# First Mlp products, its input and its first weights around the end of a planned attention stage

## The chip, the cores and the metric

The kernel runs on one core of a Trainium2 chip. The metric is the device time of one execution in microseconds (us). A core has a matrix engine (TensorE, here PE, with its weight loads shown apart as PEld), three elementwise engines (VectorE is DVE, ScalarE is ACT, GpSimd is POOL), SyncE (SP), which issues most transfers, and 16 DMA engines that carry them. Each engine runs its own instructions in order and waits for others by semaphores.

## The reference, cut to what matters

```python
q, k, v: (4, 8, 768, 48);  beta: (4, 8, 768)              # fp32
k_n = k / (norm(k) + 1e-6)
for t in range(768):                                       # delta rule, per batch and head
    y[t]  = q[t] @ state
    state = state + beta[t] * outer(k_n[t], v[t] - k_n[t] @ state)
x = y as (3072 tokens, 384)
h = x @ w_in                       # Mlp 1, 384 -> 2048
P = a0 + a1*h + a2*h^2 + a3*h^3
Q = 1 + |b0|*|h| + |b1|*h^2
x = (P / (Q + 1e-6)) @ w_out       # 2048 -> 384
h = x @ w_in2                      # Mlp 2
out = (h * tanh(log1p(exp(h)))) @ w_out2
```

## The kernel before

**Attention** goes through the 768 positions in 12 units of 64 tokens. A unit needs the inverse of a triangular 64x64 matrix per batch and head, which is reduced to 32x32 blocks; one inversion serves a pair of units, and is named here by its odd unit (1, 3, 5, 7, 9, 11). `inverse` makes it: a transposition on DVE (L534), a multiplication by rows (L538), thirty steps of one product (L552) and one addition (L558), a multiplication by columns (L580), and a second transposition on DVE (L586). `ON_DVE = (1, 9)` puts the multiplications and steps of two inversions on DVE, the other four on POOL. `prepare` loads a unit, normalises k (L449), transposes (L383), makes the Gram matrices (L398, L419) and masks them (L407, L429); L466 sets the inversion's input. `step(u)` is the recurrence itself, on the critical chain: products on PE (L690, L707, L728, L736, L751), copies out of PSUM on ACT (L714, L719, L744, L760), the rest on DVE (L698). The last products of a unit (L751) are copied (L760) and stored to `x1` by ACT's queue (L806).

**Weights.** Each Mlp has 16 blocks of 128 hidden features. An fp32 weight is split into a high and a low part for three fp32r products. A block has two sides (`w_in`, `w_out`), and each side is fetched raw (L841), then goes through `mag` on ACT (L852), `size`, `sign`, `low` on DVE (L856, L861, L867), `out` on ACT (L874) and `rest`, a subtraction on POOL (L879). A converted block is stored to DRAM (L908) and fetched again in the Mlp (L911); blocks 0 and 1 of Mlp 1 (`FQ = 2`) stay in SBUF. All 16 blocks of Mlp 1 are converted within attention.

**The plan.** Attention, the conversion, and the Mlp's first input are given to `Plan` as operations with an engine, a cost, what they read and what they write. `Plan.order` is a list scheduler: whenever an engine is free it takes the ready operation with the longest tail. `Plan.best` repeats it 2500 times with random additions to the tail of each kind of operation and keeps the best. The order found is the order of the instructions on every engine. Where the plan has a gap on PE, products of zeros are put in (L1239).

**The Mlps** run over 96 units each: 6 groups of 512 tokens (4 batches x 128 positions) by 16 blocks. `up` is nine matmuls into a PSUM bank `h` (L999); the rational function goes over ACT (L1061, L1068, L1070, L1081, L1083, L1010), DVE (L1088 to L1106) and POOL (L1064, L1074, L1014); `down` is nine matmuls four units later (L1025). The order within a unit is a written list. Group 0's input is fetched from `x1` and split into high (ACT, L979) and low (POOL, L983) parts at the end of the plan. Before the loop five blocks (`LOOK = 5`) are fetched. The conversion of eight blocks of Mlp 2 (`DIRECT = 8`) runs in Mlp 1's units by `Conv.pull`, one pull being one operation on DVE with what belongs to it on ACT, POOL and SP; its first three raw loads (`conv.start`) are issued at unit 3.

Of the kernel before, what the change touches and what calls it, by code (L numbers as in the profile page):

```python
# [9 lines left out]
F32 = mybir.dt.float32  # L10
# [12 lines left out]
HB = 16  # L23
# [3 lines left out]
DIRECT = 8  # L27
LOAD = 2700
# [17 lines left out]
CONV_START, CONV_RATE = 6, 4  # L46
# [22 lines left out]
class Plan:  # L69
# [31 lines left out]
    def order(self, bias=None):  # L101

        n = len(self.ops)
        tail, then, left = [0] * n, [[] for _ in range(n)], [0] * n
        for i in range(n - 1, -1, -1):
            engine, ns, fn, need, more, early = self.ops[i]
            tail[i] += ns + more
            left[i] = len(need)
            for j in need:
                then[j].append(i)  # L110
                tail[j] = max(tail[j], tail[i] + self.HOP)
        tail = [t - self.ops[i][5] + (bias or {}).get(self.kinds[i], 0) for i, t in enumerate(tail)]
        ready = {}
        for i in range(n):
            if not left[i]:
                ready.setdefault(self.ops[i][0], []).append((0, i))
        free, at, done = {}, [0] * n, []
        while any(ready.values()):
            best = None
            for engine, queue in ready.items():  # L120
                if queue:
                    t = max(free.get(engine, 0), min(r for r, _ in queue))
                    if best is None or t < best[0]:
                        best = (t, engine)
            t, engine = best
            queue = ready[engine]
            pick = max((x for x in queue if x[0] <= t), key=lambda x: (tail[x[1]], -x[1]))
            queue.remove(pick)
            i = pick[1]
            end = t + self.ops[i][1]  # L130
            free[engine] = end
            done.append((t, end, i))
            for j in then[i]:
                left[j] -= 1
                at[j] = max(at[j], end + self.ops[i][4] + (0 if self.ops[j][0] == engine else self.HOP))
                if not left[j]:
                    ready.setdefault(self.ops[j][0], []).append((at[j], j))
        return done

    TRIALS = 2500  # L140

    def best(self):

        def end(order):
            return max(e for _, e, _ in order)
        self.kinds = [(op[0], names[0].strip("0123456789") if names else "") for op, names in zip(self.ops, self.names)]
        kinds, rng = sorted(set(self.kinds)), random.Random(0)
        bias, order = {}, self.order()
        for _ in range(self.TRIALS):
            trial = dict(bias)  # L150
            for k in rng.sample(kinds, rng.choice((1, 2, 4))):
                trial[k] = trial.get(k, 0) + rng.gauss(0, rng.choice((1000, 5000, 20000)))
            other = self.order(trial)
            if end(other) <= end(order):
                bias, order = trial, other
        return order
# [19 lines left out]
class Attention:  # L176
# [4 lines left out]
    def __init__(self, ctx, tc, q, k, v, beta, x1, spare, spare_x):  # L181
# [17 lines left out]
        self.whole, = ring("whole", 1, [128, 2 * C])  # L199
        part, = ring("part", 1, [128, 3])  # L200
        self.top, self.bot, self.low = (part[:, i:i + 1] for i in range(3))
        self.kn = ring("kn", self.NKN, [128, M, DP])
        self.lz, self.vz = self.kn[6:]
# [9 lines left out]
        self.tmp = [flat[:, 2 * M * HC + 256 * i:2 * M * HC + 256 * i + 256] for i in range(2)]  # L213
# [1150 lines left out]
```

## Time and profile before

| | us |
|---|---|
| median of 3 runs (1089.65 to 1092.43) | 1092.06 |
| the profiled execution | 1098.82 |
| its span (first to last instruction) | 1097.1 |
| attention, to the end of its last product | 300.06 |
| first Mlp unit after which PE is without a gap | from 318.30 |

Times inside the execution count from the start of the span; 1.7 us lie outside it. In the profile's rows an instruction has its start, its duration, its engine and line, what it writes and reads, and in brackets how long the engine had been idle and what ended that.

### The profile page before, as it was taken

The numbers are of one execution on the slowest core, as the hardware profiler recorded it, in microseconds if no ns is written. First come the engines' busy times: TensorE is split into PE (matmuls) and PEld (weight loads), VectorE is DVE, ScalarE is ACT, GpSimd is POOL, SyncE is SP. The second block draws the span as 40 slices with busy tenths as digits, with TensorE's granted clock in tenths as the row PEclk, the third lists the DMA queues.
The fourth block names the chain that finished last, engine by engine and source line by source line (L and its number), as shares of the span: only waits on it lengthen the run. The fifth ranks groups of instructions, "written<-read, shape, count | busy, mean of one in ns | idle before, by whom it ended". The sixth has DMA issues, their size and how long they took to land.

```text
span 1097.1 us, 24930 instructions
## 1 busy us (share of the span) xinstructions
PE 1049.6 (96%) x10228; PEld 895.5 (82%) x10228; DVE 686.7 (63%) x1154; ACT 605.0 (55%) x1081; POOL 553.0 (50%) x640
## 2 busy tenths in 40 slices
PE   7988889988889999999999999999999999999998
PEld 6988878877768888888888888888888888888897
DVE  6886658785369999999999999882222222222211
ACT  4534645324478888989889898643232322323222
POOL 4388998186268888787888888763000000000000
PEclk9998989889899999999999999999999999999999
DMA  8727875057691121211203046340101102011010
GB/s 127 139 63 182 223 201 138 10 152 218 220 362 70 39 78 43 84 47 73 87 15 104 13 144 245 101 145 1 28 30 15 43 2 57 1 22 36 10 20 29
DMA packets 152947, 99.25 MB, mean 90 GB/s; under 512 B 114048, under 2 KB 136192, under 8 KB 152832
## 3 DMA queue, kind: packets, MB, share of 16 engines
q1 hardware_dynamic: 150976, 96.77, 31.1%
q8 instruction: 80, 1.31, 0.5%
q10 hardware_dynamic: 1600, 0.79, 0.2%
q0 software_dynamic: 256, 0.10, 0.1%
q14 instruction: 35, 0.29, 0.1%
HBM read 66.16 MB, written 31.46 MB: 89 GB/s over the span
## 4 chain that ended last, share of the span: by engine, by line
PE 83%; DVE 7%; issue 3%; POOL 3%; ACT 1%; SPq 1%; DMA 1%; DVEq 0%; POOLq 0%; ACTq 0%
PE h L999 35%; PE o L1025 33%; PE o L1039 3%; PE c_ps L707 3%; PE y_ps L751 3%; DVE xraw L552 2%; PE c_ps L728 1%; PE c_ps L690 1%; PE t_ps L383 1%; SPq L252 1%; PE s_all L736 1%; DVE s_all L558 1%; POOL x L558 1%; PE t_ps L398 1%; DVE x L558 1%
## 5 line engine op out<-in xcount | busy, mean ns | idle before, releaser
L999 PE MATMUL h<-x,w 128*128 128x512 f32 x1728 | 426.4, 391 | 4.1 <-DVE s L1090 1.9
L1025 PE MATMUL o<-gh,w 128*128 128x512 f32 x1584 | 387.6, 389 | 0.0
L999 PEld LDWEIGHTS h<-x,w 128*128 128x128 f32 x1728 | 325.0, 188 | 73.8 <-DVE s L1090 3.0
L1025 PEld LDWEIGHTS o<-gh,w 128*128 128x128 f32 x1584 | 297.3, 188 | 61.7
L1121 ACT ACTIVATE gh<-h 128x512 fp32r<-128x512 f32 x96 | 57.5, 599 | 263.1 <-PE h L999 263.1
L1014 DVE TENSOR_TENSOR gh<-g,gh 128x512 fp32r<-128x512 f32 x80 | 55.0, 687 | 232.4 <-ACT g L1126 232.4
L1014 POOL TENSOR_TENSOR gh<-g,gh 128x512 fp32r<-128x512 f32 x112 | 145.4, 1299 | 67.4 <-ACT gh L1010 45.7
L1074 POOL TENSOR_TENSOR q<-q,r 128x512 f32<-128x512 f32 x96 | 131.8, 1373 | 29.9 <-ACT r L1068 25.1
L1088 DVE TENSOR_TENSOR s<-s,h 128x512 f32<-128x512 f32 x96 | 65.3, 681 | 27.7 <-ACT s L1070 17.0
L1070 ACT ACTIVATE s<-h,ab 128x512 f32<-128x512 f32 x96 | 74.0, 771 | 5.1 <-PE h L999 5.1
L1061 ACT ACTIVATE q<-h 128x512 f32<-128x512 f32 x96 | 57.5, 599 | 35.0 <-PE h L999 34.8
L1090 DVE SCALAR_TENSOR_TENSOR s<-s,ab,h 128x512 f32<-128x512 f32 x96 | 71.8, 748 | 3.4
L1101 DVE SCALAR_TENSOR_TENSOR r<-s,ab,r 128x512 f32<-128x512 f32 x96 | 71.8, 748 | 0.0
L1106 DVE SCALAR_TENSOR_TENSOR g<-q,r 128x512 f32<-128x512 f32 x96 | 66.0, 687 | 3.3
L1081 ACT ACTIVATE r<-q,cst 128x512 f32<-128x512 f32 x96 | 66.1, 688 | 1.7 <-POOL q L1074 1.7
L558 POOL TENSOR_TENSOR x<-x,xraw 128x30 f32<-128x30 f32 (+14 forms) x120 | 62.2, 518 | 9.4
L1097 DVE SCALAR_TENSOR_TENSOR q<-q,r 128x512 f32<-128x512 f32 x96 | 65.3, 680 | 0.9 <-ACT r L1083 0.6
L879 POOL TENSOR_TENSOR w<-wm,w 128x384 fp32r<-128x384 f32 x48 | 49.6, 1037 | 32.0 <-ACT w L874 23.7
L552 POOL TENSOR_TENSOR xraw<-x 128x30 f32<-128x30 f32 (+14 forms) x120 | 60.2, 502 | 7.3
L1010 ACT CAST gh<-g 128x512 fp32r<-128x512 f32 x96 | 59.1, 616 | 0.5 <-DVE g L1106 0.5
L1083 ACT ACTIVATE r<-r 128x512 f32<-128x512 f32 x96 | 55.9, 582 | 3.1
L1126 ACT ACTIVATE g<-h 128x512 f32<-128x512 f32 x96 | 57.0, 594 | 0.0
(139 smaller groups left out, 1283.5 us busy)
## 6 DMA issues: line engine op xcount, KB each, us to landing
w<-w SPq DMA_DIRECT2D x36, 768.0 KB, 6.9
w<-in_moe_w_in_dram SPq DMA_DIRECT2D x32, 384.0 KB, 3.7
w<-in_moe_w_out_dram SPq DMA_DIRECT2D x32, 384.0 KB, 3.6
xraw<-x SPq DMA_DIRECT2D x36, 256.0 KB, 4.1
w<-wt SPq DMA_DIRECT2D x8, 768.0 KB, 3.5
kn<-in_k_dram SPq DMA_DIRECT2D x48, 96.0 KB, 3.8
qn<-in_q_dram SPq DMA_DIRECT2D x48, 96.0 KB, 4.2
v<-in_v_dram SPq DMA_DIRECT2D x48, 96.0 KB, 3.4
```

The costliest lines, as they stand in the source:

```text
L552: eng.tensor_tensor(out=tv, in0=ls[:, j, j + 1:HC].unsqueeze(1).to_broadcast([128, j, n]), in1=xs[:, 0:j, j:j + 1].to_broadcast([128, j, n ...
L558: eng.tensor_tensor(out=xs[:, 0:j, j + 1:HC], in0=xs[:, 0:j, j + 1:HC], in1=tv, op=ALU.add)
L999: self.nc.tensor.matmul(out=self.st[i]["h"], lhsT=self.w.t[f][:, a, 0, k], rhs=self.x[g][:, b, k], start=(n == 0), stop=(n == 8),)
L1014: (nc.gpsimd if engine == "P" else nc.vector).tensor_tensor(out=s["gh"][:, 1], in0=s["g"], in1=s["gh"][:, 0].bitcast(F32), op=ALU.subtract)
L1025: self.nc.tensor.matmul(out=self.acc[g][d], lhsT=self.w.t[f][:, a, 1, d], rhs=self.st[i]["gh"][:, b], start=(first and n == 0), stop=(last ...
L1070: nc.scalar.activation(out=s["s"], in_=s["h"], func=ACTF.Identity, scale=k["a3"], bias=k["a2"])
L1074: nc.gpsimd.tensor_tensor(out=s["q"], in0=s["q"], in1=s["r"], op=ALU.mult)
L1081: nc.scalar.activation(out=s["r"], in_=s["q"], func=ACTF.Ln, bias=k["c"])
L1088: nc.vector.tensor_tensor(out=s["s"], in0=s["s"], in1=s["h"], op=ALU.mult)
L1090: nc.vector.scalar_tensor_tensor(out=s["s"], in0=s["s"], scalar=k["a1"], in1=s["h"], op0=ALU.add, op1=ALU.mult)
L1101: nc.vector.scalar_tensor_tensor(out=s["r"], in0=s["s"], scalar=k["a0"], in1=s["r"], op0=ALU.add, op1=ALU.mult)
L1106: nc.vector.scalar_tensor_tensor(out=s["g"], in0=s["q"], scalar=2.0, in1=s["r"], op0=ALU.subtract, op1=ALU.mult, reverse0=True)
```

## The change

1. `Plan.best` is gone. `Plan.order` runs once, with a written table `BIAS` that is added to the tails: an entry for a kind of operation on an engine, and further ones for the same kind in one twelfth of the program.
2. The two PSUM banks of attention's `t_ps` are now the Mlp's two `h` banks, and `up` of units 0 and 1 (18 matmuls) is part of the plan, six operations of three matmuls.
3. Group 0's input no longer shares SBUF with the state copies `U`, but with the inversions' work tiles (`xs`, `tmp`), so `x_hi` and `x_lo` may run ahead of attention's end.
4. `DEFER = 2`: blocks 14 and 15 of Mlp 1 are neither converted nor stored in attention. `Conv` converts them in the Mlp's units 0 to 10 (12 pulls) straight into the tiles that the products read; its first raw loads are issued right behind the five fetches. Mlp 2's conversion starts at unit 11.
5. A way of inverting by 16x16 blocks that nothing used (`SPLIT = ()`) is removed, with its set-up: two large memsets on DVE and copies and selections of masks on POOL.

```diff
-CONV_START, CONV_RATE = 6, 4
+CONV_START, CONV_RATE = 11, 4
+BIAS = {
+    "ACT:S": -174504, "ACT:S:2": -124989, "ACT:S:3": 62305, "ACT:S:4": 130858, "ACT:S:5": 21268, "ACT:S:6": 144220,
...
+        rank = [
+            t - op[5] + BIAS.get(kind, 0) + BIAS.get(f"{kind}:{i * 12 // n}", 0)
+            for i, (t, op, kind) in enumerate(zip(tail, ops, kinds))
+        ]
...
-        for t, end, i in self.best():
+        for t, end, i in self.order():
...
-        for t in (self.vz, self.lz, *self.su):
+        for t in self.su:
             nc.vector.memset(t, 0.0)
...
+    ps.add(ctx.enter_context(tc.tile_pool(name="ps1", bufs=1, space=PSUM)), h=2)
...
-    conv = Conv([w2.convert(f, side) for f in range(NF) for side in range(2)])
+    conv = Conv(
+        [w1.convert(f, side) for f in range(NF - DEFER, NF) for side in range(2)]
+        + [w2.convert(f, side) for f in range(NF) for side in range(2)]
+    )
...
-        w1.plan(plan, [*range(FQ, NF), *range(FQ)])
+        w1.plan(plan, [*range(FQ, NF - DEFER), *range(FQ)])
...
-            plan.add("ACT", 620, lambda n=n: m1.x_hi(0, n), ["xr"], [f"x{n}", "xs0", "xs1", "U0", "U1"], early=late)
+            plan.add("ACT", 620, lambda n=n: m1.x_hi(0, n), ["xr"], [f"x{n}", "xs0", "xs1", "tmp0", "tmp1"], early=late)
             plan.add("POOL", 1300, lambda n=n: m1.x_lo(0, n), (), [f"x{n}"], early=late)
+        for n in range(2):
+            fns = m1.up(n, 0, n)
+            for j in range(0, 9, 3):
+                plan.add("PE", 690, lambda fns=fns[j:j + 3]: run(fns), [f"x{k}" for k in range(3)] + [f"w{n}"], [f"t{n}"], early=late)
...
-        fetch_w = {n: (w1.fetch_split, FQ + LOOK + n) for n in range(NF - FQ - LOOK)}
+        fetch_w = {n: (w1.fetch_split, FQ + LOOK + n) for n in range(NF - DEFER - FQ - LOOK)}
...
         for f in range(LOOK):
             w1.fetch_split(FQ + f)
+        w1.word = None
+        conv.start()
...
-        ups, downs = {}, {}
+        ups, downs = {0: [], 1: []}, {}
...
-            if i == CONV_START - 3:
-                conv.start()
...
+                elif op == "c" and i < CONV_START:
+                    conv.pull(6 * DEFER * (i + 1) // CONV_START - conv.n)
```

The lines move: `mag` is L773 after the change, `rest` L800, the raw fetch L762, the block fetch L832, `up` L920, the Mlp's `s`, `q`, `r` L991, L982, L989, its Ln and Exp L1002, L1004, the inversion's rows, steps and columns L542, L551 and L557, L561, `kn` L467, attention's y products and uu products L672 and L628.

**ACT at the start of the Mlp.** In ACT's order before, the copy and stores of the last attention output (not shown) are followed by the elementwise work of units 0, 1 and 2 (`s`, `q`, `r` from the bank `h`):

```order
L1070 ACTIVATE s<-h,ab 128x512 [waits PE_49]
L1061 ACTIVATE q<-h 128x512
L1068 ACTIVATE r<-q,ab 128x512 [waits Activation_49]
L1070 ACTIVATE s<-h,ab 128x512 [waits PE_49]
L1061 ACTIVATE q<-h 128x512
L1081 ACTIVATE r<-q,cst 128x512 [waits Pool_49]
L1083 ACTIVATE r<-r 128x512 [waits Activation_49]
```

Now, from the copy of the last attention output and its two stores on (`yst`, `x_5_65`):

```order
L681 COPY yst_159<-y_ps_164 128x8x64 [waits PE_49]
L727 DMA x_5_65<-yst_159 48x8x128 [waits Activation_49]
L727 DMA x_5_65<-yst_159 48x8x128
L991 ACTIVATE s<-h,ab 128x512
L982 ACTIVATE q<-h 128x512
L989 ACTIVATE r<-q,ab 128x512 [waits Activation_49]
L773 ACTIVATE wm<-w_4950 128x384 [waits DMAHW2_49]
L991 ACTIVATE s<-h,ab 128x512 [waits PE_49]
L982 ACTIVATE q<-h 128x512
L1002 ACTIVATE r<-q,cst 128x512 [waits Pool_49]
L1004 ACTIVATE r<-r 128x512 [waits Activation_49]
L773 ACTIVATE wm<-w_4952 128x384 [waits DMAHW3_49]
```

A `mag`, which waits for a transfer's landing, stands now between unit 0's and unit 1's work, and a second one behind unit 0's Exp.

**SP at attention's end.** Before, five block fetches stand there (`w_2` to `w_6`), then three that wait on further transfers, and the raw loads of Mlp 2's first block behind a fourth:

```order
L911 DMA w<-w_5_85 128x1536 [waits DMAHW6_49]
L911 DMA w<-w_6_86 128x1536 [waits DMAHW7_49]
L911 DMA w<-w_7_87 128x1536 [waits DMAHW0_49]
L911 DMA w<-w_8_88 128x1536 [waits DMAHW1_49]
L911 DMA w<-w_9_89 128x1536 [waits DMAHW2_49]
L841 DMA w_5083<-in_moe_w_in_dram 128x3x128 [waits DMAHW3_49,PE_49]
L841 DMA w_5085<-in_moe_w_out_dram 128x384 [waits DMAHW4_49,DVE_49,Activation_49]
L841 DMA w_5087<-in_moe_w_in_dram 128x3x128 [waits DMAHW5_49,DVE_49,Activation_49]
```

Now (the raw tiles `w_4950`, `w_4952`, `w_4954` are those of blocks 14 and 15 of Mlp 1):

```order
L832 DMA w<-w_5_88 128x1536 [waits DMAHW0_49]
L832 DMA w<-w_6_89 128x1536 [waits DMAHW1_49]
L762 DMA w_4950<-in_moe_w_in_dram 128x3x128 [waits DMAHW2_49,PE_49]
L762 DMA w_4952<-in_moe_w_out_dram 128x384 [waits DMAHW3_49,DVE_49]
L762 DMA w_4954<-in_moe_w_in_dram 128x3x128 [waits DMAHW4_49,DVE_49,Activation_49]
L832 DMA w<-w_7_90 128x1536 [waits DMAHW5_49]
L832 DMA w<-w_8_91 128x1536 [waits DMAHW6_49]
L832 DMA w<-w_9_92 128x1536 [waits DMAHW7_49]
```

The raw loads moved ahead of three block fetches. A DMAHW semaphore is shared in turn by all transfers of SP and ACT, so these waits are for the transfer that had it before: in the changed program that is for `w_6` the first of ACT's last four stores of attention's output, for the first raw load the second store, for the other two the third and fourth; before, `w_7` was the first that waited for one of these stores.

**POOL from the inversion of units 6 and 7 to that of units 10 and 11.** Before, the one ends and the other begins, and subtractions of the conversion stand among the steps further on:

```order
L580 TENSOR_TENSOR x<-x 128x1024 [waits Pool_49]
L538 TENSOR_TENSOR x<-x 128x1024 [waits DVE_49]
L546 MEMSET x 128x32 [waits Pool_49]
L552 TENSOR_TENSOR xraw<-x 128x30
...
L552 TENSOR_TENSOR xraw<-x 128x184 [waits Pool_49]
L558 TENSOR_TENSOR x<-x,xraw 128x8x23 [waits Pool_49]
L879 TENSOR_TENSOR w<-wm,w 128x384 [waits Activation_49]
L552 TENSOR_TENSOR xraw<-x 128x198 [waits Pool_49]
```

Now:

```order
L561 TENSOR_TENSOR x<-x 128x1024 [waits Pool_49]
L800 TENSOR_TENSOR w<-wm,w 128x384 [waits Activation_49]
L800 TENSOR_TENSOR w<-wm,w 128x384 [waits DMAHW3_49,Activation_49]
L467 TENSOR_TENSOR kn_130<-kn_130,xraw 128x16x48 [waits DMAHW1_49,DMAHW0_49,DMAHW7_49,DVE_49,PE_49]
L467 TENSOR_TENSOR kn_131<-kn_131,xraw 128x16x48 [waits DMAHW5_49,DMAHW6_49,DMAHW4_49,DMAHW7_49,PE_49,Activation_49]
L542 TENSOR_TENSOR x<-x 128x1024 [waits DVE_49]
L545 MEMSET x 128x32 [waits Pool_49]
L551 TENSOR_TENSOR x<-x 128x30
```

Two subtractions and the normalisation of units 10 and 11 stand between the two inversions; within the last one there are seven subtractions before and none now.

## Rows read from the trace of the kernel before

**Rows 1.** Windows: length, busy PE, PEld, DVE, ACT, POOL, granted clock, DMA share, GB/s.

```profile
140.70:176.07 35.37, 32.36 (x921) 28.98 (x919) 21.48 (x49) 19.59 (x39) 32.35 (x55) 0.90 0.70 173
196.90:213.60 16.70, 16.70 (x420) 15.22 (x420) 10.86 (x29) 7.39 (x13) 0.00 (x0) 0.73 0.01 3
264.65:300.06 35.41, 29.79 (x872) 28.14 (x868) 15.26 (x28) 13.70 (x29) 6.09 (x7) 0.82 0.67 212
318.30:648.00 329.70, 329.70 (x1456) 272.99 (x1456) 308.20 (x467) 294.95 (x503) 268.93 (x223) 1.00 0.20 71
```

**Rows 2.** Timeline of all engines from attention's end to the Mlp's fifth unit.

```profile
298.96 1.10 PE L751 MATMUL y_ps<-gm,x 64*48 64x64 f32 x32
...
301.72 0.58 ACT L760 COPY yst<-y_ps 128x512 f32<-128x512 f32 x1
...
302.33 0.97 ACTq L806 DMA_DIRECT2D x<-yst  x2
...
306.61 0.78 ACT L1070 ACTIVATE s<-h,ab 128x512 f32<-128x512 f32 x1 [4.31 <-PE h L999]
...
309.43 1.92 PEld L999 LDWEIGHTS h<-x,w 128*128 128x128 f32 x9 [0.34 <-DVE s L1090]
...
309.54 0.78 ACT L1070 ACTIVATE s<-h,ab 128x512 f32<-128x512 f32 x1 [0.82 <-PE h L999]
...
315.96 2.33 PE L999 MATMUL h<-x,w 128*128 128x512 f32 x9 [1.26 <-DVE s L1090]
```

**Rows 3.** DVE's timeline: the transpositions that begin and end inversions.

```profile
138.69 2.03 DVE L586 STREAM_TRANSPOSE xt<-x 128x1024 f32<-128x1024 f32 x1 [1.12 <-POOL x L580]
...
176.07 2.01 DVE L534 STREAM_TRANSPOSE x<-lg 128x1024 f32<-128x1024 f32 x1 [0.43 <-ACT lg L466]
...
213.64 1.97 DVE L534 STREAM_TRANSPOSE x<-xraw 128x1024 f32<-128x1024 f32 x1
...
236.40 1.94 DVE L586 STREAM_TRANSPOSE xt<-x 128x1024 f32<-128x1024 f32 x1
...
262.70 1.95 DVE L586 STREAM_TRANSPOSE xt<-x 128x1024 f32<-128x1024 f32 x1
```

**Rows 4.** Groups of POOL's instructions from 47 to 263 us.

```profile
L879 POOL TENSOR_TENSOR w<-wm,w 128x384 fp32r<-128x384 f32 x25 | 25.0, 1000 | 1.7 <-ACT w L874 1.6
...
L449 POOL TENSOR_TENSOR kn<-kn,nrm 128x768 f32<-128x768 f32 x6 | 8.7, 1479 | 0.9 <-DVE nrm L375 0.8
```

**Rows 5.** Groups of DVE's instructions from 176 to 238.4 us.

```profile
L552 DVE TENSOR_TENSOR xraw<-x 128x30 f32<-128x30 f32 (+14 forms) x30 | 17.2, 574 | 0.7
L558 DVE TENSOR_TENSOR x<-x,xraw 128x30 f32<-128x30 f32 (+14 forms) x30 | 14.3, 477 | 1.0
...
L698 DVE TENSOR_TENSOR r<-r,c_ps 128x384 f32<-128x384 f32 x4 | 2.2, 549 | 5.0 <-PE c_ps L728 5.0
...
L861 DVE SCALAR_TENSOR_TENSOR word<-wm,word 128x384 int32<-128x384 int32 x2 | 1.1, 556 | 0.0
```

**Rows 6.** Conversion in Mlp 1's units: a `mag` on ACT.

```profile
333.56 0.55 ACT L852 ACTIVATE wm<-w 128x384 f32<-128x384 f32 x1
```

**Rows 7.** The same on DVE: a `sign`.

```profile
340.18 0.84 DVE L861 SCALAR_TENSOR_TENSOR w<-wm,w 128x384 int32<-128x384 int32 x1
```

**Rows 8.** Transfers issued from 297 to 299.9: count, size, us to landing.

```profile
x<-yst ACTq DMA_DIRECT2D x2, 192.0 KB, 9.1
```

**Rows 9.** Transfers issued from 301.5 to 304.

```profile
x<-yst ACTq DMA_DIRECT2D x2, 192.0 KB, 5.9
```

**Rows 10.** Transfers issued from 305 to 312.

```profile
w<-in_moe_w_in_dram SPq DMA_DIRECT2D x2, 384.0 KB, 10.4
```

**Rows 11.** Raw loads of the whole execution, from the page.

```profile
w<-in_moe_w_in_dram SPq DMA_DIRECT2D x32, 384.0 KB, 3.7
```

**Rows 12.** SP's waits from 293 to 312: total, times, longest.

```profile
SPq L911 <- DMA x<-yst: 11.2, 4, 10.5
```

**Rows 13.** DVE's first work on the data, behind the set-up's memsets.

```profile
7.43 0.95 DVE L350 TENSOR_REDUCE nrm<-gm 128x16 f32<-128x768 f32 x1 [0.86 <-ACT gm L346]
```

More of the change, by code (lines that the diff above doesn't have):

```diff
@@ L99, in add, with order @@
         self.ops.append((engine, ns, fn, sorted(need), more, early))
-    def order(self, bias=None):
-        n = len(self.ops)
-        tail, then, left = [0] * n, [[] for _ in range(n)], [0] * n
+    def order(self):
+        ops, n = self.ops, len(self.ops)
+        kinds = [f"{op[0]}:{names[0].strip('0123456789') if names else ''}" for op, names in zip(ops, self.names)]
+        tail, then = [0] * n, [[] for _ in range(n)]
         for i in range(n - 1, -1, -1):
[L106 to L109, printed above, removed]
+            tail[i] += ops[i][1] + ops[i][4]
+            for j in ops[i][3]:
@@ L114, in order @@
+        later, now, free = ({e: [] for e in engines} for _ in range(3))
+        free = dict.fromkeys(engines, 0)
         for i in range(n):
             if not left[i]:
[L116 to L131, printed above, removed]
+                heapq.heappush(later[ops[i][0]], (0, i))
@@ new lines, in order @@
+        done = []
+        while len(done) < n:
+            t, engine = min(
+                ((free[e] if now[e] else max(free[e], later[e][0][0]), e) for e in engines if now[e] or later[e]),
+                key=lambda x: x[0],
+            )
+            while later[engine] and later[engine][0][0] <= t:
+                i = heapq.heappop(later[engine])[1]
+                heapq.heappush(now[engine], (-rank[i], i))
+            i = heapq.heappop(now[engine])[1]
+            end = free[engine] = t + ops[i][1]
@@ L138, in order @@
         return done
[L140 to L156, printed above, removed]
@@ L427, in spread @@
             n, part = cols.stop - cols.start, slice(M // 2 * d, M // 2 * d + M // 2)
[L428 removed]
+            mask = self.mask[:, cols]
             return lambda: nc.vector.tensor_tensor(
@@ L622, in join_out @@
[L622 to L630 removed]
+        whole = 2150 if engine == "POOL" else 1230
         p.add("DVE", 2000, first, [f"{lgb}{j}{i}" for j in range(2) for i in range(4)], lsb)
@@ L634, in inverse @@
             p.add("ACT", 1020, lambda: nc.scalar.copy(out=xs, in_=ls), lsb, xsb)
-        p.add(engine, 500 if split else 150, ones, (), xsb)
-        for j in range(1, size - 1):
-            n = HC // size * j * (size - 1 - j)
+        p.add(engine, 150, diag, (), xsb)
+        for j in range(1, HC - 1):
+            n = j * (HC - 1 - j)
             cost = 3.7 * n + 480 if engine == "POOL" else 2.1 * n + 340 if early else 4.2 * n + 300
```

166 lines of the change are left out of this document (29 added, 137 removed), and 52 rows, old and new, of the table BIAS.

## The prediction, made before the changed kernel ran

> **What bounds the kernel now.** I read the windows first, to see where PE is the limit. From 318.30 us on PE is busy in all of the 329.70 us looked at, at full clock [rows 1]; it stays so to the end, 1456 matmuls in 329.70 us, 0.226 us each, 18 to a unit: 4.08 us. DVE is the next with 308.20 of the same 329.70. The change does not touch these products, so whatever it is worth must bring the start of this stretch forward. That start has two parts: the end of attention's last product, and the hand-over from there.
>
> Attention was read in the same windows, and in DVE's timeline of the transpositions. Its chain is an alternation. A unit's recurrence can't begin before its inversion is there; the inversion of units 8 and 9 (on DVE) begins at 176.07, and its result is there at 236.40 + 1.94 = 238.34; that of units 10 and 11 (on POOL) begins on DVE at 213.64 and ends at 262.70 + 1.95 = 264.65 [rows 3]. From there the last two units need 35.41 us, in which PE is busy for 29.79 at a mean granted clock of 0.82 [rows 1]. Earlier stretches are fuller still: PE busy 32.36 of 35.37 at 0.90, and 16.70 of 16.70 at 0.73 [rows 1].
>
> The hand-over was read in the timeline. The last product of attention ends at 298.96 + 1.10 = 300.06. The third unit's products begin 9.37 later (309.43), the fifth's 15.9 later (315.96), and from there on PE has no gap that matters [rows 2]. In between the chain is: split the input, two units' products, then ACT and DVE work per unit before a bank `h` is free.
>
> **The change, part by part.** The sum is made against the profiled execution, 1098.82 us; the median of the runs is 1092.06, 0.6% less, so a difference is carried over as a share.
>
> *Attention, the inversions.* I compared each engine's order between the ends of inversions. POOL: seven subtractions leave the last inversion (7 x 1.00 [rows 4] = -7.0) and three join the stretch that ends with the second POOL inversion (+3.0); the third one loses three subtractions and two normalisations, 3.0 + 2 x 1.48 = 6.0 [rows 4], which only move behind it. DVE: between the end at 138.69 and the beginning at 176.07 one conversion operation fewer (0.556), within the fifth inversion three fewer, -1.7; ahead of the first transposition of units 10 and 11 six more of the inversion's operations, (574 + 477)/2 = 526 ns each, and two more rests of 0.549 [rows 5]: +3.2 + 1.1 = +4.2.
>
> If all waits stay, the fifth inversion ends at 238.34 + 3.0 - 0.6 - 1.7 = 239.0, and the transposition at 213.64 comes at 213.64 + 3.0 - 0.6 + 4.2 = 220.2. POOL then needs what it needed, 262.70 - (213.64 + 1.97) = 47.1, less 7.0: it ends at 220.2 + 2.0 + 40.1 = 262.3 and its transposition at 264.3: nothing gained. The order may however win back what PE loses in these stretches, and PE bounds that: in 140.70 to 176.07 it idles 3.0 and loses 35.37 x 0.10 = 3.5 to the clock, in 196.90 to 213.60 it loses 16.70 x 0.27 = 4.5 [rows 1]; 11.0 in all. The order alone does not say how much of it comes back. I take half, 5.5, with 0 and 11 as the ends: the fifth inversion ends at 233.5, the last one at 258.8. Two units follow the fifth inversion's end before the last one's result is used, 264.65 - 238.34 = 26.3 [rows 3]: 259.8. So the last two units start 4.9 earlier.
>
> *Products within attention.* Of the 18 matmuls that move, 12 stand ahead of attention's last product, 12 x 0.226 = 2.7. The stretch has 35.41 - 29.79 = 5.6 of idle PE [rows 1], so from none to all of it is hidden; a little under half, since in the new order half of the 12 stand between products that already wait for ACT, leaves +1.5. Attention's end: -4.9 + 1.5 = -3.4.
>
> *Hand-over without a new wait.* The last stores' copy would be at +0.1, copy and two stores take 302.33 + 0.97 - 301.72 = 1.58, and unit 0's `s` follows at +1.7, since its product is done. From there to the third unit's product it took 309.43 - 306.61 = 2.82 [rows 2]: +4.5 in place of +9.37. From that same `s` to the fifth unit's product it took 315.96 - 306.61 = 9.35 [rows 2].
>
> *The new wait.* Behind unit 0's `s`, `q` and `r` on ACT there is now a `mag` that waits for the first raw load of block 14. Behind it stand unit 1's `s` and everything after it; DVE's `size` of the same side stands between unit 0's two first products, and behind it unit 1. Call L the landing of that load, counted from attention's end. Unit 1's `s` starts at L + 0.55 [rows 6], the fifth unit's product 315.96 - 309.54 = 6.42 later [rows 2], and a `sign` of 0.84 [rows 7] stands in the way on DVE: L + 7.8, where before it was 15.9. The hand-over changes by L - 8.1.
>
> What is L? SP issues the raw load only after the semaphore before it is free, that is when the second of the last four output stores has landed. These stores are the pair issued ahead of the last copy. Before, their copy starts 2.7 before attention's end; now six of the moved matmuls (1.4) and a group of about 1.0 (as the 1.10 of [rows 2]) stand in between, so it is 5.1 before the end, and the stores are issued at -4.4 and -4.0. Before, the like pair landed 9.1 after its issue [rows 8], with five block fetches under way. The price of a block fetch ahead I take from raw loads: 10.4 behind three fetches [rows 10] against 3.7 as a median [rows 11], 2.2 each. In the new order the fifth fetch itself waits for the first store, so there are four ahead: 9.1 - 2.2 = 6.9. The second store lands at +2.9, the raw load is issued at +3.3 behind that fetch, and lands 3.7 + 2.2 = 5.9 later: L = 9.2, the hand-over +1.1. The ends: stores that land in 5.9, as the later pair did [rows 9], and a load in 3.7 give L = 2.3 + 3.7 = 6.0, so -2.1; 9.1 and 10.4 give L = 5.5 + 10.4 = 15.9, so +7.8. That such a wait is real is seen before: SP stood 11.2 us for these stores, 10.5 at once [rows 12], but there only fetches of blocks needed much later were queued behind it.
>
> A variant of its own, E: the store takes 9.1 however many fetches stand ahead, since ACT's stores and SP's fetches share the transfer engines in equal turns; [rows 8] is as well explained by that as by a price per fetch, and no row shows four fetches. Then the load is issued at +5.5 and L = 5.5 + 5.9 = 11.4: the hand-over +3.3, the sum -0.1, 1092. The Trainium skill has this as a rule ("DMA: Bandwidth & Descriptors", Queues, rings and completion order): SP and ACT own one queue row each, and every DMA engine takes turns between rows, a packet at a time. The trace agrees in so far as 9.1 is longer than the 5.9 of the pair behind; by the rule the sum would be -0.1, by a price per fetch -2.3.
>
> *The rest.* The conversion in units 0 to 10 is 12 operations on DVE in 11 units, by the sizes above about 0.6 to 0.8 a unit. DVE has (329.70 - 308.20)/80.8 units = 0.27 free per 4.08 us, with the old conversion's 0.5 or so already in it, so it is just full there; it costs nothing as long as a bank `h` comes free a little ahead of PE, and at most 11 x 0.3 = 3 if not. I take 0. The memsets taken out of the set-up are hidden, because DVE idles 0.86 before its first work, waiting for ACT [rows 13]: 0. The four stores and fetches of blocks 14 and 15 that fall away load no engine that is waited for: 0.
>
> Sum: -3.4 + 1.1 = -2.3 on 1098.82, 0.21%, so 1089.7 as a median.
>
> **The rivals.**
>
> *A. The order wins nearly all.* The clock in the rows of attention rises, and the last two units' gaps are filled by the moved products. Then 11 instead of 5.5 come back, and the 1.5 isn't paid: -2.3 - 5.5 - 1.5 = -9.3; with the clock's loss in the tail too (35.41 x 0.18 = 6.4 [rows 1]) -15.7. For it: PE loses in each of these stretches, and the new products are full-size ones that can go anywhere. Against it: half of the loss stands between waits of a serial chain. Time 1076 to 1083.
>
> *B. The raw load lands late (the other side).* If the stores really wait out the whole fetch traffic and the load too, L is near 15.9, the hand-over +7.8, the sum +4.4: 1096.4. It decides against the change from L = 8.1 + 3.4 = 11.5 on, and is beyond the bound of measurement from L = 14.8. For it: [rows 8, 10]. Against it: only four fetches stand ahead of the store, and none behind the load until the third store has landed.
>
> *C. The order wins nothing.* Attention goes as in the sum without the 5.5: the fifth inversion at +0.6, the moved products +1.5, the hand-over +1.1, together +3.2, or more where the inversion operations that moved ahead of the last transposition (+4.2 on DVE) delay it further: 1095 to 1097. For it: 8 of the 11 us are the clock's [rows 1], which a new order need not raise. Against it: PE idles too.
>
> *D. No stall.* If the load lands by +3.8, when ACT gets to it (`s` at 1.7, two more instructions by the spacing of [rows 2], 309.54 - 306.61 less 0.82 of waiting), the hand-over gives 3.8 + 7.8 - 15.9 = -4.3: the sum is -7.7, 1084.4. It needs the stores to land before attention ends.
>
> **How the numbers follow.** What a measurement of this kernel can tell from no change is about 0.3%, 3.3 us. The forecast has 0.35, and by itself reaches from 1083 to 1096 (the ends of what comes back, of the load and of the 1.5): 0.18 of it faster, 0.13 the same, 0.04 slower. A has 0.25, faster. B has 0.12, of which 0.09 slower and 0.03 the same. C has 0.12, 0.08 slower and 0.04 the same. D has 0.08, faster. E has 0.08: 0.02 faster, 0.06 the same. Together faster 0.53, same 0.26, slower 0.21. The range must reach into A and to B and C on the other side: 1076 leaves out about 0.10 of A's longer end, 1098 about 0.08.
>
> **What would show it.** Attention's last product should end about 3.4 earlier, near 296.7, with the last inversion's transposition near 260 or earlier. The Mlp's third unit should start some 4.5 after that end, and unit 1's `s` should be seen waiting for a DMA, up to about 9.2 after it; the fifth unit's product near +17. The stretch after it should be as before, 4.08 a unit without a gap, the first 11 units too. The prediction is wrong if attention's end moves by more than 8 either way, if the wait for the raw load is absent or longer than 12, or if PE shows gaps in the units with the new conversion.

## The result and the profile after

The changed kernel takes 1099.41 us (median of 4 runs, 1098.42 to 1100.38), the kernel before beside it 1092.24 (4 runs, 1089.65 to 1093.68): a ratio of 1.0068, 95% interval 1.004 to 1.0096. In a second job it was 1101.1 (five runs) and 1.0083 (1.0053 to 1.0113). The change makes the kernel slower by 0.7 to 0.8%, where a gain of 0.2% was forecast; the time lies just above the range of 1076 to 1098. Three single executions far longer than all others (1693.54, 2255.56 and 3585.79 us, the last a traced one) are left out of the times here, so the changed kernel has one trace. The jobs ran on several chips, on which the kernel before had medians from 1091.91 to 1093.36, so runs of different jobs are compared by their ratios to it.

The trace that the prediction was made from turned out to be a long execution of before: 1098.82 us, where 25 runs of a later job have a median of 1093.36. So the kernel before was traced again (label before_again, 1094.05 us), and the changed kernel is read against that trace. Four landmarks tell where the time lies: the end of attention's last product; the start of the fifth unit's products (PE has no long gap from there); that of the seventeenth unit; the end. From the seventeenth unit to the last product all traces below take the same 727.8 us.

| | before, [rows 1 to 3] | before, second trace | after | after - second trace |
|---|---|---|---|---|
| attention's last product ends | 300.1 | 294.3 | 298.4 | +4.1 |
| to the fifth unit's products | 15.9 | 16.9 | 16.1 | -0.8 |
| fifth to seventeenth unit | 49.1 | 49.1 | 51.4 | +2.3 |
| after the last product | 4.2 | 4.2 | 5.0 | +0.8 |
| span | 1097.1 | 1092.3 | 1098.7 | +6.4 |

The first windows are the changed kernel's (columns as in [rows 1]); they run from the beginning of the fifth inversion to the end of the fourth, attention's last two units, the hand-over, and the fifth to the seventeenth unit.

```profile
180.40:199.20 18.80, 11.91 (x244) 11.13 (x240) 13.29 (x26) 4.09 (x9) 13.58 (x20) 0.77 0.32 89
268.20:298.40 30.20, 27.20 (x813) 24.14 (x814) 15.61 (x30) 14.27 (x30) 10.66 (x10) 0.94 0.80 258
298.40:314.50 16.10, 9.43 (x24) 6.48 (x25) 7.18 (x12) 9.52 (x16) 4.24 (x4) 0.75 0.99 349
314.50:365.90 51.40, 50.63 (x218) 41.19 (x218) 50.53 (x74) 45.90 (x78) 43.28 (x38) 0.98 0.30 108
```

The same four in the second trace of before:

```profile
176.10:197.80 21.70, 16.73 (x314) 15.11 (x314) 20.87 (x38) 6.97 (x14) 14.96 (x23) 0.92 0.36 86
260.80:294.30 33.50, 27.20 (x866) 25.48 (x862) 15.26 (x28) 13.79 (x29) 6.16 (x7) 0.91 0.71 220
294.30:311.20 16.90, 12.87 (x39) 8.59 (x37) 6.33 (x10) 10.41 (x18) 8.57 (x8) 0.80 0.96 345
311.20:360.30 49.10, 49.10 (x217) 40.65 (x218) 46.05 (x70) 43.76 (x74) 41.33 (x35) 1.00 0.36 138
```

In the first stretch PE is busy in 11.9 of 18.8 us after the change, before in 16.7 of 21.7, and its granted clock is 0.77, against 0.92. In the last one DVE's busy time grows from 46.05 of 49.1 to 50.53 of 51.4: it has nothing left. The transpositions on DVE, answering to [rows 3], show attention losing before its last two units: the last inversion begins at 223.96 and is there at 268.2, against 210.3 and 260.8 in the second trace of before.

```profile
180.41 1.98 DVE L539 STREAM_TRANSPOSE x<-lg 128x1024 f32<-128x1024 f32 x1 [0.47 <-ACT lg L484]
...
223.96 1.95 DVE L539 STREAM_TRANSPOSE x<-xraw 128x1024 f32<-128x1024 f32 x1 [0.39 <-ACT xraw L484]
...
266.21 2.00 DVE L564 STREAM_TRANSPOSE xt<-x 128x1024 f32<-128x1024 f32 x1 [6.03 <-POOL x L561]
```

The timeline of the changed kernel near 190 us shows what happens there:

```profile
183.64 0.84 ACT L364 ACTIVATE gm<-kn 128x768 f32<-128x768 f32 x1
...
188.38 1.91 POOL L561 TENSOR_TENSOR x<-x 128x1024 f32<-128x1024 f32 x1
...
190.25 1.95 POOL L800 TENSOR_TENSOR w<-wm,w 128x384 fp32r<-128x384 f32 x2
...
191.28 0.55 ACT L773 ACTIVATE wm<-w 128x384 f32<-128x384 f32 x1 [6.79 <-POOL w L800]
191.73 0.21 ACT L382 ACTIVATE xraw<-xraw 128x32 f32<-128x32 f32 x1
191.97 0.23 ACT L383 ACTIVATE xraw<-xraw 128x32 f32<-128x32 f32 x1
192.11 0.46 ACT L665 COPY su<-s_all 128x384 f32<-128x384 f32 x1
192.24 0.35 DVE L387 RECIPROCAL xraw<-xraw 128x32 f32<-128x32 f32 x1 [4.14 <-ACT xraw L383]
...
192.62 1.65 PE L1164 MATMUL s_all<-zero 128*128 128x128 f32 x6 [6.81 <-ACT su L665]
193.78 2.95 POOL L467 TENSOR_TENSOR kn<-kn,xraw 128x768 f32<-128x768 f32 x2 [1.58 <-issue]
```

Read from the top: ACT is idle for 6.79 us, because the next instruction in its order is a `mag` of the weights' conversion. Its buffer `wm` is free only after a subtraction on POOL (L800), and that stands behind POOL's third inversion. Behind the `mag` on ACT stand the roots of units 10 and 11's normalisation (L382, L383) and the copy of the state (L665). So DVE waits 4.14 us for the root, PE 6.81 us for the state, and the normalisation (L467) ends at 193.78 + 2.95 = 196.7; before the change it ran inside the inversion.

The hand-over, on ACT and PE (it answers to [rows 2]):

```profile
299.90 0.78 ACT L991 ACTIVATE s<-h,ab 128x512 f32<-128x512 f32 x1 [0.92 <-ACT yst L681]
...
302.72 3.91 PE L920 MATMUL h<-x,w 128*128 128x512 f32 x9 [2.78 <-DVE s L1011]
307.27 0.54 ACT L773 ACTIVATE wm<-w 128x384 f32<-128x384 f32 x1 [5.26 <-DMA w<-in_moe_w_in_dram]
...
310.53 7.26 PE L920 MATMUL h<-x,w 128*128 128x512 f32 x18 [3.90 <-DVE s L1011]
```

The third unit starts 4.4 after attention's end, not 9.4, and then ACT waits 5.26 us for the deferred block's raw load, as was written.

### The profile page after: what moved, and what is told of

The parts are those of the page before. It is cut to its first block, busy times and chain, and to the rows that moved or that the text cites. A ratio compares the mean times of both kernels' runs of the same rounds, so it can differ in the third digit from the quotient of the medians.

```text
span 1098.7 us, 24884 instructions
## 1 busy us (share of the span) xinstructions
PE 1045.5 (95%) x10226; PEld 890.3 (81%) x10226; DVE 685.5 (62%) x1152; ACT 604.9 (55%) x1081; POOL 551.8 (50%) x625
## 4 chain that ended last, share of the span: by engine, by line
PE 70%; DVE 4%; POOL 3%; DMA 2%; ACT 1%; issue 1%; ACTq 0%; DVEq 0%; SPq 0%; POOLq 0%
PE h L920 33%; PE o L946 31%; PE o L960 3%; POOL x L557 1%; POOL x L551 1%; DMA w<-in_moe_w_out_dram 1%; DMA x<-yst 1%; DVE g L1027 1%; DVE q L1018 1%; DVE r L1022 1%; DVE wm L788 1%; PE y_ps L672 0%; DVE s L1009 0%; DMA w<-in_moe_w_in_dram 0%; PE c_ps L611 0%
## 5 line engine op out<-in xcount | busy, mean ns | idle before, releaser
L920 PE MATMUL h<-x,w 128*128 128x512 f32 x1728 | 429.0, 393 | 7.4 <-DVE s L1011 7.4
L920 PEld LDWEIGHTS h<-x,w 128*128 128x128 f32 x1728 | 326.5, 190 | 77.2 <-DVE s L1011 9.7
L991 ACT ACTIVATE s<-h,ab 128x512 f32<-128x512 f32 x96 | 74.0, 771 | 1.5 <-ACT yst L681 0.9
L982 ACT ACTIVATE q<-h 128x512 f32<-128x512 f32 x96 | 57.4, 598 | 28.3 <-PE h L920 28.0
L557 POOL TENSOR_TENSOR x<-x 128x30 f32<-128x30 f32 (+14 forms) x120 | 63.0, 525 | 9.4
L1002 ACT ACTIVATE r<-q,cst 128x512 f32<-128x512 f32 x96 | 66.1, 688 | 0.6 <-POOL q L995 0.5
L551 POOL TENSOR_TENSOR x<-x 128x30 f32<-128x30 f32 (+14 forms) x120 | 59.1, 492 | 8.0
L800 POOL TENSOR_TENSOR w<-wm,w 128x384 fp32r<-128x384 f32 x48 | 49.7, 1041 | 20.9 <-ACT w L795 20.9
L1004 ACT ACTIVATE r<-r 128x512 f32<-128x512 f32 x96 | 55.9, 582 | 3.1
```

The lines of the kernel that those rows point to most:

```text
L551: eng.tensor_tensor(out=tv, in0=ls[:, j, j + 1:HC].unsqueeze(1).to_broadcast([128, j, n]), in1=xs[:, 0:j, j:j + 1].to_broadcast([128, j, n ...
L557: eng.tensor_tensor(out=xs[:, 0:j, j + 1:HC], in0=xs[:, 0:j, j + 1:HC], in1=tv, op=ALU.add)
L920: self.nc.tensor.matmul(out=self.st[i]["h"], lhsT=self.w.t[f][:, a, 0, k], rhs=self.x[g][:, b, k], start=(n == 0), stop=(n == 8),)
L991: nc.scalar.activation(out=s["s"], in_=s["h"], func=ACTF.Identity, scale=k["a3"], bias=k["a2"])
L1002: nc.scalar.activation(out=s["r"], in_=s["q"], func=ACTF.Ln, bias=k["c"])
```

## The experiments

**The kernel before, traced again.** No edit.

> The kernel before, unchanged, for a second trace of it. The profiled execution of before took 1098.82 us where its timed runs have a median near 1092, so its trace is some 6 us longer than what the change is timed against. Theory 1 (the order): this trace shows attention ending near 294 instead of 300.06, with the hand-over and the units behind as they were; the changed kernel's 298.4 is then 4 us later, not 1.7 earlier. Theory 2 (the new wait): attention ends near 300 again, and the 6 us are found elsewhere. Time 1092 by both.

1092.97 us (median of 10 runs), ratio 0.9997 (0.998 to 1.0013); its 25 companions reach from 1088.79 to 1101.82. Attention ends at 294.3: theory 1's number. The last transposition of the inversions is over at 260.8 against 264.65 in [rows 3], the tail is 33.5 against 35.4.

**The table alone on the kernel before.** Its `Plan.best` is replaced by the new `Plan.order` and `BIAS`.

```diff
...
-        for t, end, i in self.best():
+        for t, end, i in self.order():
```

> The kernel before with Plan.order and the table of the change, nothing else. Theory 1 (the table's order makes attention longer): slower by 3 to 6 us, 1095 to 1098, attention's last inversion ending 3 or more later. Theory 2 (the new wait for the deferred block's raw load makes the change slower): no change beyond 2 us, 1090 to 1094. The table was written for another graph with two blocks fewer, so its twelfths fall a little elsewhere; a much worse time says nothing on theory 1.

1100.76 (4 runs), 1.0073 (1.0055 to 1.0091), but not by theory 1: attention's last product ends at 292.2, earlier than before. PE then stands for 12.78 us, as the conversion of block 0 is not done:

```profile
304.94 1.62 PE L1039 MATMUL h<-x,w 128*128 128x512 f32 x3 [12.78 <-DVE wm L907]
```

The table fits only the graph that it was written for. This run says nothing for or against theory 1.

**The search in place of the table on the changed kernel**, with the old `Plan.order` that it repeats.

```diff
...
-        for t, end, i in self.order():
+        for t, end, i in self.best():
```

> The changed kernel with the old random search in place of the table, nothing else. Theory 1: attention's end comes 4 us or more earlier than 298.4, total 1093 to 1096. Theory 2: the wait for the raw load is still there, 1098 to 1101.

1095.13 (nine runs; 1095.99 with the tenth, of 1693.54), 1.0033 (1.0011 to 1.0054): about half of the loss is the order's. In the trace, which is of its fastest execution (1094.5), attention ends at 291.1, the hand-over is 17.4, the stretch behind 51.5. The losses in the hand-over and behind it are there without the table.

**The deferred conversion two units later.**

```diff
-CONV_START, CONV_RATE = 11, 4
+CONV_START, CONV_RATE = 13, 4
...
-                    conv.pull(6 * DEFER * (i + 1) // CONV_START - conv.n)
+                    conv.pull(6 * DEFER * max(0, i - 1) // (CONV_START - 2) - conv.n)
```

> The changed kernel with the deferred conversion's 12 pulls in units 2 to 12 instead of 0 to 10 (CONV_START 13), so that ACT's first mag stands behind units 0 and 1 and part of unit 2; raw loads are issued where they were. Theory 2: unit 1's s no longer waits 5.3 us, the fifth unit's product comes 3 to 5 us earlier, 1094.5 to 1096.5. Theory 1: attention ends at 298.4 as before; the hand-over's gain is the same 3 to 5, and what stays above 1092 is attention's. Rival: the work is merely put off, and the wait shows up as PE gaps in units 3 to 12: 1099.

1098.71 (10 runs, 1096.19 to 1106.05), 1.0057 (1.0025 to 1.0088): the hand-over falls from 16.1 to 10.0, the stretch behind grows from 51.4 to 53.6. The rival has part of it: the stall's time is won, a third of it lost again to a full DVE (busy in 52.83 of 53.7 us). Attention ends at 300.3 in this trace, 1.9 later than in the changed kernel's, so of the 1094.5 to 1096.5 expected little is seen.

**The raw loads ahead of two block fetches**, with the table and with the search.

```diff
...
+        w1.word = None
         for f in range(LOOK):
+            if f == 3:
+                conv.start()
             w1.fetch_split(FQ + f)
-        w1.word = None
-        conv.start()
...
```

> The changed kernel with the three first raw loads issued ahead of the fourth and fifth block fetch instead of behind the fifth, so that the first of them no longer waits for a store of attention's output; the pulls stay in units 0 to 10. If the stall of ACT for that load (5.3 us) is what the hand-over costs, the fifth unit's product comes 4 us earlier after attention's end (11.7 to 12.5 instead of 16.1) and the kernel takes 1095 to 1096. Rival: DVE is so full with the conversion in these units that it gives the time back by unit 16 (from the fifth unit to the seventeenth 53 us instead of 51.4): 1097 to 1099.

1095.4 (9 runs), 1.0024 (0.9997 to 1.0052), where the changed kernel had 1.0068. The hand-over is 10.9, ACT no longer waits for the load, and the stretch behind takes 52.8. The `mag` and the next `s` in its trace:

```profile
298.69 0.78 ACT L991 ACTIVATE s<-h,ab 128x512 f32<-128x512 f32 x1 [0.91 <-ACT yst L681]
300.71 0.53 ACT L773 ACTIVATE wm<-w 128x384 f32<-128x384 f32 x1
301.15 0.76 ACT L991 ACTIVATE s<-h,ab 128x512 f32<-128x512 f32 x1
```

> The same edit on the changed kernel with the old search. By the first theory 4 us less than the 1095.99 without the edit: 1091 to 1093. By the rival 1094 to 1096.

1089.9 (nine runs), 0.9996 (0.9976 to 1.0017): by the ratios 0.37%, 4 us, less than the search alone, and level with before. Hand-over 11.4, stretch 52.4. So the wait is real and worth 4 to 5 us; the stretch behind gives back 0.9 to 1.4 in the traces.

**Without the deferred conversion, and without the moved products** (both with the search). The first has `DEFER = 0`, `CONV_START = 6` and the raw loads at unit 3, the second leaves out the six `plan.add` of `up`.

> The changed kernel with the old search and DEFER = 0 (all 16 blocks converted in attention, CONV_START 6 and the raw loads at unit 3 as before): what is left of the change is the input and the two units' products within attention. If the deferred conversion is what costs (the stall at the hand-over, 2.3 us of full DVE in units 4 to 16), the hand-over is 10 to 12 us after attention's end, units 4 to 16 take 49.1, and with attention ending at 292 to 295 the kernel takes 1085 to 1088, less than before. If the moved products and the two blocks lengthen attention by as much as they save, 1091 to 1094.

1091.98 (10 runs, 1084.52 to 1098.61), 0.9994 (0.9963 to 1.0025). The stretch behind is 49.3, as expected, but attention ends at 296.3, the first unit's products start at 296.2, and the hand-over is 13.3, not 10 to 12: in the order that the search found with 16 blocks to convert, the moved products don't come ahead of attention's end. Nothing is won or lost.

> The changed kernel with the old search and without the two units' products in attention (they are made at the start of the Mlp, as before); the deferred conversion and the early input stay. If deferring the two blocks shortens attention by itself, it ends at 287 to 290, the hand-over is longer than 17 us, with ACT waiting for the raw load, and the kernel takes 1094 to 1097. If deferring wins nothing in attention, 1097 to 1100.

1098.8 (6 runs), 1.0069 (1.0039 to 1.0099). Its trace is of its longest execution (1103.51); there attention ends at 295.5, later than expected, and the hand-over is 22.0 with ACT waiting 9.89 us for the raw load. As the stall differs too, this run doesn't isolate what the moved products are worth.

**The one `mag` moved.** In the changed kernel, one entry of the plan's list is moved before the list is issued.

```diff
...
+        root = max(k for k, kind in enumerate(kinds) if kind in ("ACT:nrm0s", "ACT:nrm1s"))
+        prev = max(k for k in range(root) if kinds[k].startswith("ACT:"))
...
+        state = min(k for k in range(root, len(kinds)) if kinds[k] == "ACT:S")
+        done.insert(state, done.pop(prev))
...
```

> The changed kernel with one instruction moved: the mag on ACT that stood ahead of the roots of the last normalisation and of a copy of the state (it waited 6.8 us for a subtraction on POOL behind the inversion of units 6 and 7) comes right behind that copy. Theory (the table's order costs what ACT's wait costs): the 6.8 us of PE's idling near 185 to 192 go, the first transposition of units 10 and 11 comes 4 to 8 earlier than 224, attention ends at 291 to 295, the kernel takes 1093 to 1096. Rival (the order as a whole is worse, this wait is covered by the inversion on DVE): attention ends at 297 or later, 1098 to 1100.

1097.45 (12 runs, 1090.99 to 1103.87), 1.0029 (1.0002 to 1.0055), above the 1093 to 1096 expected. The traced execution was its fastest, with attention's end at 288.7. It was repeated beside the changed kernel.

> The changed kernel unchanged, for a second trace and more times beside its variant with the moved mag on the same chip. If its four first times (1098.4 to 1100.4) are typical, it lies at 1098 to 1101 with ACT's wait of 5 us or more in the trace near 190; if it scatters as the variant did, 1091 to 1104 with a median near 1098.

1101.1 (median of five, 1100.32 to 1105.26), ratio 1.0083 (1.0053 to 1.0113), without a second trace.

> The variant with the one mag moved, again. Its trace was that of its fastest execution (1091, attention's end 288.7), its median 1097.5. If the moved instruction is what makes attention shorter, this trace shows attention's end at least 3 us ahead of the changed kernel's in the same job, and the median 3 to 6 us lower. Rival: the first trace was a lucky execution, and both kernels agree within 2 us.

1097.13 (12 runs), 1.0038 (1.0012 to 1.0064): 4.0 us less than the changed kernel in the same job. The two intervals touch, but each of the changed kernel's five times is longer than ten or more of the twelve. Attention ends at 292.8, 5.6 ahead of the changed kernel's one trace. In this trace the `mag` still waits, but nothing that others need stands behind it:

```profile
186.46 0.46 ACT L672 COPY su<-s_all 128x384 f32<-128x384 f32 x1
186.97 0.94 PE L1171 MATMUL s_all<-zero 128*128 128x128 f32 x6 [1.06 <-ACT su L672]
189.68 0.56 ACT L780 ACTIVATE wm<-w 128x384 f32<-128x384 f32 x1 [2.76 <-POOL w L807]
...
191.39 2.96 POOL L474 TENSOR_TENSOR kn<-kn,xraw 128x768 f32<-128x768 f32 x2 [0.79 <-issue]
```

The last inversion begins at 218.8 in place of 224.0. One trace of each would be little, but `raw_early` and `late_conv` have the changed kernel's plan too: in these three traces the last inversion begins at 222.1 to 224.2, in the four with the `mag` moved (with the two variants below) at 216.3 to 218.8. In `late_conv` ACT idles only 2.33 us ahead of that `mag`, and yet the copy of the state comes at 191.3, not near the 186.5 above: it is late by what POOL still has to do, however long or short ACT stands idle for that. The theory on the cause holds, and this one instruction's place makes 4 us.

> The mag moved and the raw loads early, without the thinned pulls. If the causes add up, the early raw loads take 3.5 to 4.5 off the variant with the mag alone (0.4% between the changed kernel and its variant with the early loads alone): near 1093, and the thinned pulls give the rest to 1090.9.

1092.14 (12 runs), 0.9999 (0.9978 to 1.0021): 5 us less than with the `mag` alone in the same job. The two causes add up, within the intervals.

**All three.** Besides, the normalisation's products go ahead of the two subtractions on POOL, both `mag`s behind the next copies `kq`, and the pulls are thinned (the edit of the list and of `CONV_START` isn't shown):

```diff
...
-                    conv.pull(6 * DEFER * (i + 1) // CONV_START - conv.n)
+                    conv.pull((9 * (i + 1) // 11 if i < 11 else max(9, i - 4)) - conv.n)
```

> The changed kernel with that mag and its follower behind the next transposition's copies, the last normalisation's products ahead of the two subtractions on POOL, the raw loads ahead of the fourth block fetch, and the deferred conversion's pulls thinned out: 9 in units 0 to 10, none in units 11 to 13, where group 1's input is split, and the last 3 in units 14 to 16. If the three causes add up: attention ends near 292, the hand-over is 11, the fifth to the seventeenth unit 50 to 51, the kernel takes 1086 to 1089, less than before. If DVE stays the limit whatever the spread, 52.5 and 1089 to 1091; if the moved mag wins nothing, 1092 to 1095.

1090.88 (12 runs), 0.997 (0.9948 to 0.9992). The stretch behind the hand-over is 50.2 and the hand-over 12.0, about as expected, but attention ends at 295.5 in this trace, not near 292, and the time is above the 1086 to 1089 expected. The stretch:

```profile
307.50:357.70 50.20, 49.81 (x216) 40.40 (x217) 49.37 (x72) 46.16 (x79) 43.35 (x37) 1.00 0.37 142
```

> The changed kernel with the old search, the early raw loads and the same thinned pulls. If the pulls' number per unit makes the 52.4 us from the fifth to the seventeenth unit, it becomes 50 to 51 and the kernel takes 1087 to 1089; if it is the single long operations beside POOL, it stays 52 or more and the kernel near 1090.

1089.03 (12 runs), 0.996 (0.9938 to 0.9982), with attention's end at 293.0, the hand-over 10.8 and the stretch 50.2, against 52.4 without the thinning; in time the thinning is no more than 0.36%, with intervals that overlap. This beats both kernels, by 0.4% and (1.0068 / 0.996) 1.1%; in the search's order a `mag` waits up to 5.9 us for POOL as well, but no wait of PE for a state copy comes of it.

## Why the prediction was wrong

*Attention's end: -3.4 forecast, +4.1 measured.* The step that failed is the one on POOL's order: two normalisations of 1.48 us "which only move behind" the third inversion. They were taken as POOL time alone. The rows of the order shown ahead of the prediction had them behind two subtractions; what wasn't asked is who waits for them, and what stands ahead of the roots on ACT. Units 10 and 11's Gram matrices hang on them, and with them the last inversion, whose beginning was put at 214.7 (220.2 with nothing won back) and came at 224.0. The cause is the `mag` on ACT, shown by moving it: 1.0083 becomes 1.0038 in one job, and attention's end in its trace is 292.8, 1.5 ahead of before's second trace. "I take half, 5.5" of PE's loss as won back had no ground in this order; with the `mag` where it was, nothing came back. What POOL's order gives in the last inversion was forecast rightly: 40.3 us from transposition to transposition (40.1 forecast), against 46.5 in the second trace of before. The 1.5 for the moved products wasn't seen: attention's last two units take 30.2, against 33.5 and 35.4.

*The hand-over: +1.1 forecast; measured -0.8 against the second trace, +0.2 against the first.* The steps came as forecast: `s` at +1.55 (1.7 forecast), the third unit at +4.4 (4.5), the load landing at 307.27 - 298.35 = +8.9 (9.2), the fifth unit at +16.1 (17.0). SP's waits and the two landings:

```profile
SPq L832 <- DMA x<-yst: 9.3, 1, 9.3
```

```profile
x<-yst ACTq DMA_DIRECT2D x2, 192.0 KB, 8.2
```

```profile
w<-in_moe_w_in_dram SPq DMA_DIRECT2D x2, 384.0 KB, 5.6
```

The price of L rested on a wrong count, and that it came out near is partly luck. SP's four waits in [rows 12] are for the four stores, one each; behind them the fifth to the eighth block fetch were issued, from 307.01 on. So `w_6`, not `w_7`, was already the first to wait for a store before the change; four fetches, not five, stood ahead of the pair of [rows 8], and four, not three, ahead of the raw load of [rows 10]. So the price would have been 1.7 a fetch, not 2.2, and taking it off the 9.1 for one fetch fewer had no ground. The stores took 8.2 with four fetches ahead, and 9.1 before with as many. In both traces the first of them lands right behind the last of these fetches (301.37 and 301.13 now, 307.00 and 306.74 before), and with three ahead (`raw_early`) the pair took 6.4 and 7.2. So E's condition, the same time however many fetches stand ahead, is not what the traces show, although the queues do take turns; the last section has why.

That an L of 9 makes the wait cost nearly everything that the early products bring, the forecast didn't say plainly: without it the hand-over is 10 to 12, and that is 4 to 5 us of the time.

*The Mlp's first units: 0 forecast, bound 3, measured +2.3.* The term was mis-sized. Twelve operations cost (1277 + 826 + 458)/3 = 854 ns each, not 0.6 to 0.8:

```profile
L788 DVE SCALAR_TENSOR_TENSOR wm<-w 128x384 int32<-128x384 int32 x4 | 5.1, 1277 | 0.0
L782 DVE SCALAR_TENSOR_TENSOR w<-wm,w 128x384 int32<-128x384 int32 x4 | 3.3, 826 | 0.0
L777 DVE TENSOR_SCALAR w<-wm 128x384 int32<-128x384 int32 x4 | 1.8, 458 | 5.2 <-ACT wm L773 5.2
```

Unit by unit, from one unit's first product to the next one's, the loss has three places. The first is not DVE's: the fifth unit takes 5.2 where before it took 4.2 (+0.9), at a low granted clock. From 310.5 to 317 it was 0.52, nearly all at the lower level (1.2 of 2.4 GHz), where before's second trace has 1.00 from 311.2 to 315.4; PE had been busy 5.46 of the 12.1 us ahead, with gaps.

```profile
310.50:317.00 6.50, 6.47 (x16) 4.92 (x17) 6.40 (x11) 5.78 (x11) 4.01 (x4) 0.52 0.57 235
```

The second is one place with two conversion operations in a row, since 12 pulls go into 11 units. From the thirteenth unit to the fourteenth (348.25 to 353.27) it takes 5.0 in place of 4.08:

```profile
348.84 1.29 DVE L782 SCALAR_TENSOR_TENSOR w<-wm,w 128x384 int32<-128x384 int32 x1
350.16 1.67 DVE L788 SCALAR_TENSOR_TENSOR wm<-w 128x384 int32<-128x384 int32 x1
353.27 2.33 PE L920 MATMUL h<-x,w 128*128 128x512 f32 x9 [0.77 <-DVE s L1011]
```

The last 0.4 is in the two units behind, in which DVE splits group 1's input. The sixth to the twelfth unit take 4.08 as before, at one operation a unit. Thinning the pulls takes the double one away: that place takes 5.5 in `search_raw_early` and 4.08 in `search_raw_spread`, the stretch 52.4 and 50.2.

*The base.* A difference was carried over as a share from an execution 6 us above the median. The trace's attention was 5.8 longer than the second one's, so whatever was worked out from its rows was worked out from a poor specimen. The trace itself gave no sign which execution it was, but the table of times did: 1098.82 lay outside the three runs' range.

*After the last product* 0.8 us more are seen in the one trace (0.3 to 1.2 in its variants). Why stays open; no run was made for it.

*The rivals.* The stall came at the sum's size (L 8.9), not at rival B's 15.9. Rival C's total, 1095 to 1097, came nearest, but for another reason: attention didn't just fail to win, it got a wait.

## What to carry to other kernels

When a priority table reorders engines, look on each in-order engine for an instruction of side work (here a weight's conversion) whose buffer is freed by another engine's long job, and list what of the main chain stands behind it; here one such instruction cost 4 us. Work deferred from one stage into another needs its loads issued clear of slow neighbours in the queue, and room on the engine that it goes to, by durations taken beside that engine's real company and unit by unit: here most of DVE's part of the loss came from the one place with two operations in a row. How many transfers stand ahead of another is read from the times of issue, not from the order in the program alone. Before a trace is used as a base, its own time should lie within the spread of the runs.

## What the runs showed of the hardware

**DVE and POOL.** One operation on DVE (L788) took 0.55 or 1.66 us by what POOL did. In the changed kernel's trace, DVE beside POOL:

```profile
316.21 0.55 DVE L788 SCALAR_TENSOR_TENSOR wm<-w 128x384 int32<-128x384 int32 x1
316.22 1.19 POOL L985 TENSOR_SCALAR r<-q,ab 128x512 f32<-128x512 f32 x1
...
327.88 1.28 POOL L995 TENSOR_TENSOR q<-q,r 128x512 f32<-128x512 f32 x1
327.92 1.66 DVE L788 SCALAR_TENSOR_TENSOR wm<-w 128x384 int32<-128x384 int32 x1
...
350.12 1.30 POOL L935 TENSOR_TENSOR gh<-g,gh 128x512 fp32r<-128x512 f32 x1 [0.41 <-ACT gh L931]
350.16 1.67 DVE L788 SCALAR_TENSOR_TENSOR wm<-w 128x384 int32<-128x384 int32 x1
```

The one that starts later, by 0.01 to 0.04 us, is drawn out: DVE's 1.66 ends 0.42 after POOL's end, and at 316.22 POOL's L985 takes 1.19, where it takes 0.77 when DVE is out of its way (353.44 in the same trace). In attention, with `word` in PSUM, the same DVE operations took 0.55 to 0.56 in the mean. The Trainium skill ("SBUF — State Buffer", Who interferes with whom) says that a DVE instruction with two inputs in SBUF and a POOL instruction that reads SBUF block one another, the second to issue until the first is done; these rows agree.

**Two queues on the transfer engines.** From 297 to 299.5 in the changed kernel's trace, SP's queue (q1, block fetches) and ACT's (q10, stores of attention's output) both have work. Packets, MB, busy share:

```profile
q1 hardware_dynamic: 142, 0.77, 89.5%
q10 hardware_dynamic: 126, 0.06, 8.5%
```

16 of the 142 are under 512 B; of the rest each queue has 126, so they take turns packet by packet, which agrees with the rule of the Trainium skill that the prediction names ("DMA: Bandwidth & Descriptors", Queues, rings and completion order). But a fetch's packet carries about 6 KB and a store's about 0.5 KB, so the store gets a twelfth or so of the bytes while a fetch has any left, and lands right behind the last of the fetches ahead of it. So here equal turns come to a price per fetch.

**The spread.** Executions of the kernel before on one chip spread over 1.2% (1088.79 to 1101.82 in 25 runs). Between two traces of it the difference lay in attention, 300.1 against 294.3; the hand-over was 1.0 the other way, 15.9 against 16.9, and 49.1 and 727.8 behind it were the same.
